# Sums and differences before the first stage, and the forward stage in bursts of 64x64 tiles

## The chip, the cores and the metric

The kernel runs on one core of a Trainium2 chip. The metric is the device time of one execution in microseconds (us), the median of several runs. Engines: TensorE (PE in the profile, its weight loads PEld), VectorE (DVE), ScalarE (ACT), GpSimd (POOL) and SyncE (SP); POOL and SP mostly issue DMA transfers here.

## The reference

Two parts follow one another. The first filters a sequence in the frequency domain, the second is a two-layer network with an exact GELU.

```python
X = np.fft.rfft(x, axis=1)                    # x: 8 batches, 3008 steps, 256 channels
Y = X * (filt_r + 1j * filt_i)[None]
y = np.fft.irfft(Y, n=3008, axis=1)
h = y.reshape(24064, 256) @ w_in              # 256 -> 2048
g = 0.5 * h * (1.0 + erf(h / sqrt(2)))
out = g @ w_out                               # 2048 -> 256
```

Inputs and output are fp32; the kernel works in bf16 and fp16 with fp32 sums in PSUM.

## The kernel before

**The transform.** 3008 = 47 x 64, so both transforms are done as small matrix products in two steps each. A step index is n = 64 n1 + 32 h + w. Per batch there are four stages on TensorE.

- s1 (lines 386 to 413): the sum over n1 (47 terms), one call for each quarter c of the 32 values of w. Its matmuls are 47 rows by 64 columns, so four of them, on two row halves and two column halves of the array, can stand side by side. Four PSUM banks are evicted into `a_sb`, which goes to DRAM (`R1`) and comes back in another order (r1).
- s2 (lines 421 to 431): the forward sum over the 64 values of (h, w), with the weights T2p. 24 matmuls of 128x128x256 per batch, two of them in each of 12 units p. VectorE multiplies each unit's PSUM bank by the filter F (line 430), real and imaginary part, and writes a tile `p12`.
- s3 (lines 434 to 458): the first inverse stage, 16 matmuls of 64x64x512 for each group u of four units, evicted to `v_sb` and turned through DRAM (`R2`, r2).
- s4 (lines 468 to 485): the last inverse stage; 16 calls per batch write the filtered sequence into a ring of two batches, `y_sb`.

Batch 0 goes another way, by transposes on chip (c1 to c4), in a start-up of about 39 us.

**The network.** 47 tiles of 512 tokens, each in 16 slots. In a slot, `mm1` (line 583) does two matmuls of 128x128x512 into a bank `ps_h` (three banks, which s1 and s3 also take one of), and ScalarE evicts it with GELU (line 595). `mm2_seven` does the second product of the tile before with seven instead of eight block products (Strassen's method): seven matmuls of 128x128x128 per slot into `ps_o` (two banks, line 665), 112 per tile in the order m = 0 to 6 of the block products, 16 each. VectorE prepares sums of quarters of g for it (`sums_1`, line 634, in slots 12, 13, 15 and 17; `sums_2`, line 640, in slots 16 and 18; `sums_3`, line 647, in slots 21 and 24, counted from the tile's own start) and combines the block products into the output (lines 680 to 694, after m = 0, 2, 4 and 6). A matmul of m = 2 needs sums_2: the 33rd matmul of a tile the first half, the 37th (slot 5) the second.

**Order.** The order is written out by hand: a table `at` puts each spectral call of batches 1 to 7 at a slot, and the loop at the end walks the slots and emits first the slot's table entries, then mm2, then mm1. Every engine executes in that order. For batches 3 to 6, with hi the first slot in which the batch is needed, s1 begins at hi - 94 and s2's units lie at about every third slot from hi - 70, with the three s3 bursts between them. Within one slot, entries stand in the order in which they were put: spectral calls of an earlier batch first, and the sums last.

**x.** One buffer holds x of a batch; GpSimd loads the next batch into it in eight transfers, each held back by a small copy (`gate`) that reads a product of s2.

Of the kernel before, what the change touches and what calls it, by code (L numbers as in the profile page):

```python
# [14 lines left out]
I32 = mybir.dt.int32  # L15
# [16 lines left out]
class _Mix:  # L32
    def __init__(self, ctx, tc, x, filt_r, filt_i, w_in, w_out, out):
# [12 lines left out]
        self.pp = pool("pp", 6)  # L46
# [11 lines left out]
        self.T2p = c.tile([128, K1, 2, 2, 2, 16], BF16, name="T2p")  # L58
# [20 lines left out]
    def load_x(self, b, lo=0, n=32, hs=(0, 1)):  # L79
        nc = self.nc  # L80
        if lo == 0 and 0 in hs:
            self.st[b, "x"] = self.px.tile([128 if b else 2 * NA, HB, 256], BF16, tag="x", name="x_sb")
        xt, o = self.st[b, "x"], 64 if b else NA
        xv = self.x[b].rearrange("(n1 h w) d -> h n1 w d", h=2, w=HB)
        for w in range(lo, lo + n, 8):
            for h in hs:
                nc.gpsimd.dma_start(out=xt[h * o:h * o + NA, w:w + 8, :], in_=xv[h][:, w:w + 8, :])  # L87

# [20 lines left out]
    def load_filters_again(self, eng, k0, k):  # L109

        for o in range(0, 128, 32):
            i = self.st["Fd"][o // 64, :, :, :, k0:k0 + k, :].rearrange("q i t k c -> (q i) t (k c)")
            eng.dma_start(out=self.F[o:o + 32, :, k0:k0 + k, :], in_=i)
# [11 lines left out]
    def load_next(self, b, p, c, h):  # L125

        if b > 0:
            self.gate(self.st[b, "p", p][0:1, 0, 0:1])
        self.load_x(b + 1, 8 * c, 8, (h,))
# [41 lines left out]
    def table_2_rows(self, g):  # L171


        v = self.nc.vector
        ts = v.tensor_scalar
        col = lambda name, dt=FP32: g.tile([128, 1], dt, name=name)
        ri_i, h_i, w_i = col("ri_i", I32), col("h_i", I32), col("w_i", I32)
        ts(out=h_i, in0=self.pi, scalar1=1, scalar2=1, op0=ALU.logical_shift_right, op1=ALU.bitwise_and)
        ts(out=w_i, in0=self.pi, scalar1=2, scalar2=None, op0=ALU.logical_shift_right)
        ts(out=ri_i, in0=self.pi, scalar1=1, scalar2=None, op0=ALU.bitwise_and)  # L180
        self.n2, self.ri = col("n2"), col("ri")
        v.scalar_tensor_tensor(out=self.n2, in0=h_i, scalar=float(HB), in1=w_i, op0=ALU.mult, op1=ALU.add)
        ts(out=self.n2, in0=self.n2, scalar1=1.0 / self.S, scalar2=None, op0=ALU.mult)
        ts(out=self.ri, in0=ri_i, scalar1=-0.25, scalar2=TURNS + 0.25, op0=ALU.mult, op1=ALU.add)
# [40 lines left out]
    def weights_4(self, g):  # L225

        ts = self.nc.gpsimd.tensor_scalar
        h, q, self.wt, self.wts = (g.tile([128, 1], FP32, name=n) for n in ("h48", "q48", "wt", "wts"))
        ts(out=h, in0=self.p, scalar1=48.0, scalar2=None, op0=ALU.is_ge)
        ts(out=q, in0=h, scalar1=-48.0, scalar2=-1.0, op0=ALU.mult, op1=ALU.add)  # L230
        self.nc.gpsimd.tensor_tensor(out=q, in0=self.p, in1=q, op=ALU.add)
        self.nc.gpsimd.tensor_tensor(out=q, in0=q, in1=q, op=ALU.mult)
        ts(out=q, in0=q, scalar1=1.0, scalar2=-1.0, op0=ALU.is_equal, op1=ALU.mult)
# [43 lines left out]
    def table_3_copy(self, q, turn):  # L277

        k = slice(8 * q, 8 * q + 8)
        if turn < 2:  # L280
            self._evac(self.T3[:, k], self.t3.rearrange("p (k w e) -> p k e w", k=8, e=4), "act")
        if turn:
            v = self.t3.rearrange("p (k w h r) -> p k h r w", k=8, h=2, r=2)
            for r in range(2):
                self._evac(self.T3i[:, k, r::2, :], v[:, :, :, 1 - r, :], "act", self.turn[r])

    def table_3_turn(self, q):

        k = slice(8 * q, 8 * q + 8)
        for r in range(2):  # L290
            self.nc.vector.tensor_scalar(out=self.T3i[:, k, r::2, :], in0=self.T3[:, k, 1 - r::2, :],
# [27 lines left out]
    def table_2_parities(self):  # L319
        t = self.T2.rearrange("p k r (s j e) -> p k r s j e", s=2, e=2)  # L320
        for par in range(2):
            for q in range(2):
                self.nc.gpsimd.tensor_copy(out=self.T2p[:, :, par, :, q, :], in_=t[:, :, :, q, :, par ^ q])

    def table_u_rows(self, g):
# [3 lines left out]
        v.tensor_copy(out=self.u0[:, 0], in_=self.T3[:, 0, 0:2, :])  # L329
        v.tensor_copy(out=self.u0[:, 1], in_=self.T3i[:, 0, 0:2, :])  # L330
# [14 lines left out]
    def table_4_rows(self, g):  # L345
# [5 lines left out]
        for x in range(2):  # L351
            for r in range(2):
                t = self.T1[0:NA, 24 * (x ^ r):24 * (x ^ r) + 24].rearrange("p (a k) -> p a k", k=2)
                v.tensor_copy(out=self.T1g[:, x, r], in_=t.unsqueeze(2).to_broadcast([NA, 12, 2, 2]))
        t = self.T2.rearrange("p (a k) r j -> p r a j k", k=2)[:, 0, :, 0:2, :]
        for r in range(2):
            v.tensor_copy(out=self.T2g[:, r], in_=t)

    def table_4_factors(self, g):
# [7 lines left out]
        self.fcs = t[:, 96:224].rearrange("p (w h r) -> p w h r", h=2, r=2)  # L367
# [16 lines left out]
    def s1(self, b, c):  # L384
# [4 lines left out]
        if b == 1 and c == 3:  # L389
            a = [self.pp.tile([128, 2, 512], BF16, tag="p12", name="p12") for i in range(2)]  # L390
        else:
            at = self.pa.tile([128, 4, 512], BF16, tag="a", name="a_sb")
            a = [at[:, 0:2], at[:, 2:4]]
        x = self.st[b, "x"]
        ps = [[self.bank("ps_s1", "h" if i == h == 0 else "f") for h in range(2)] for i in range(2)]
        for i in range(2):
            for r in range(2):
                for h in range(2):
                    w = 8 * c + 4 * r + 2 * i
                    nc.tensor.matmul(ps[i][h][64 * r:64 * r + 64, :], lhsT=self.T1s[64 * h:64 * h + NA],  # L400
                                     rhs=x[64 * h:64 * h + NA, w:w + 2, :], start=True, stop=True)
        for i in range(2):
            for h in range(2):
                self._evac(a[i][:, :, 256 * h:256 * h + 256], ps[i][h].rearrange("p (w c) -> p w c", w=2),
                           "act" if h and (b > 1 or i) else False)
        o = self.st[b, "R1"].rearrange("(w h) q c -> q w h c", h=2)
        for r in range(2):
            w, q = 8 * c + 4 * r, slice(64 * r, 64 * r + 48)
            if b == 1 and c == 3:
                for i in range(2):  # L410
                    nc.sync.dma_start(out=o[:, w + 2 * i:w + 2 * i + 2], in_=a[i][q].rearrange("q w (h c) -> q w h c", h=2))
            else:
                nc.sync.dma_start(out=o[:, w:w + 4], in_=at[q].rearrange("q w (h c) -> q w h c", h=2))
# [8 lines left out]
    def s2(self, b, p):  # L422
        nc = self.nc
        ps = self.bank("ps_s2")
        for i in range(2):
            k = 2 * p + i
            nc.tensor.matmul(ps[:, 256 * i:256 * i + 256], lhsT=self.T2p[:, k].rearrange("p a b c d -> p (a b c d)"),  # L427
                             rhs=self.st[b, "b", k // 6][:, k % 6, :], start=True, stop=True)
        w = self.st[b, "p", p] = self.pp.tile([128, 2, 512], BF16, tag="p12", name="p12")
        nc.vector.tensor_tensor(out=w, in0=ps.unsqueeze(1).to_broadcast([128, 2, 512]),  # L430
                                in1=self.F[:, :, 2 * p:2 * p + 2, :].rearrange("p t a b -> p t (a b)"), op=ALU.mult)
# [18 lines left out]
    def s3_out(self, b, u, i):  # L450
        ps = self.st[b, "ps3"][i]
        vt = self.pv.tile([128, 4, 256], BF16, tag="v", name="v_sb")
        for par in range(2):
            self._evac(vt[:, 2 * par:2 * par + 2, :].rearrange("p a b -> p (a b)"), ps[par],
                       "act" if par or b < 3 else False)
# [30 lines left out]
    def c1(self, grp, half, eng):  # L486

        if grp == 0 and half == 0:
            n = 4 * K1 * 2 * HB
            self.at = self.y0[:, 4608:4608 + n].rearrange("c (a k n h r) -> c a k n h r", a=2, k=K1, h=2, r=2)  # L490
        ps = self.bank("ps_c1", "n")
        x = self.st[0, "x"]
        for i in range(4):
            self.nc.tensor.matmul(ps[:, 96 * i:96 * i + 96], lhsT=x[:, 4 * grp + i, 128 * half:128 * half + 128],
                                  rhs=self.T1c, start=True, stop=True)
        self._evac(self.at[:, half].rearrange("c k n h r -> c k n (h r)")[:, :, 4 * grp:4 * grp + 4, :],
                   ps[:, 0:384].rearrange("c (i k e) -> c k i e", i=4, e=4), eng)

    def c1t(self, q, eng):
# [3 lines left out]
        for i in range(8):  # L503
            self.nc.tensor.transpose(ps[:, 128 * i:128 * i + 128],
                                     self.at[:, i % 2, 4 * q + i // 2].rearrange("c n h r -> c (n h r)"), self.eye)
# [4 lines left out]
    def c2(self, p):  # L510

        nc = self.nc
        w = self.st[0, "p", p] = self.pp.tile([128, 2, 512], BF16, tag="p12", name="p12")
# [220 lines left out]
def kernel(  # L734
# [20 lines left out]
    m.load_x(0, 0, 8)  # L755
    m.k48 = m.iota(g, "k48", [128, 2, K1], [[0, 2], [1, K1]])
    m.load_x(0, 8, 8, (0,))
# [5 lines left out]
    m.load_x(0, 8, 8, (1,))  # L763
    cols = m.cols = m.iota(g, "cols", [128, 128], [[1, 128]])
    m.load_x(0, 16, 16)
# [11 lines left out]
    t3 = m.pg.tile([128, 2, K1, 4, HB], BF16, tag="g", name="T3")  # L777
# [10 lines left out]
    for u in range(16):  # L788
        m.c1(u // 2, u % 2, False if u in (1, 3, 5, 7, 8, 10, 12, 14) else act)
        if u == 3:  # L790
# [4 lines left out]
            nc.vector.tensor_copy(out=m.T1q, in_=m.T1.rearrange("p (h r k) -> p k h r", h=2, r=2))  # L795
# [47 lines left out]
    m.load_x(1)  # L843
# [23 lines left out]
    for b in range(1, B):  # L867
        hi = first(b)
        if b == 1:
            s1, n1, r1, s2, n2, group = 0, 3, 12, 28, 3, 14  # L870
        elif b == 2:
            s1, n1, r1, s2, n2, group = hi - 87, 3.7, hi - 73, hi - 64, 3.4, 14
        else:
            s1, n1, r1, s2, n2, group = hi - 94, 3.7, hi - 80, hi - 70, 3.4, 14
        unit = lambda p: s2 + group * (p // 4) + int(n2 * (p % 4))
        busy.update(range(s1 - 1, s1 + int(3 * n1) + 2))
        for c in range(4):
            put(s1 + int(c * n1), m.s1, b, c)
            put(r1 if c < 3 else unit(3) + 1, m.r1, b, c)
        for p in range(12):  # L880
            put(unit(p), m.s2, b, p)
            busy.add(unit(p))
            if p % 4 == 3:
                put(unit(p) + 3, m.s3, b, p // 4)
                put(unit(p) + 4, m.s3_out, b, p // 4, 1)
                busy.update(range(unit(p) + 2, unit(p) + 6))
        after[b] = unit(11) + 7
        crowd.update(range(s2, after[b]))
        if b + 1 < B:
            for i in range(8):  # L890
                put(unit(i + 2), m.load_next, b, i + 2, i // 2, i % 2)

    for b in range(1, B):
# [8 lines left out]
        for u in range(7, -1, -1):  # L902
            due = (b * S + GRP * u) // TCH * 16
            end = min(end, due - 2 + 6 * (u == 0 and b == 1))
            for half in (1, 0):
                while end in busy:
                    end -= 1
                assert end > after[b] + 8
                put(end, m.s4, b, u, half, act if half or end in crowd or b == 1 and u == 0 else False)
                busy.add(end)  # L910
                end -= 2
            if u % 2 == 0:
                put(after[b] if u == 0 else end - 8, m.r2, b, u // 2)
# [65 lines left out]
```

## Time and profile before

| | |
|---|---|
| time, median of 3 runs | 745.92 us (745.81 to 746.71) |
| span of the profiled run | 745.3 us |
| PE busy | 728.5 us (98%) |
| DVE busy | 573.2 us (77%) |
| ACT busy | 557.5 us (75%) |
| POOL busy | 227.7 us (31%) |
| chain that ended last, share of PE | 91% |

Busy time is the union of an engine's instructions over the span. Rows of a group read: line, engine, operation, output and inputs, shape, count, then busy time, mean length of one in ns, and the engine's idle time before them with what ended it. TensorE's matmuls are pipelined: a matmul of 512 columns is recorded with 379 ns, but the next one starts 216 ns later. So the starts, not the lengths, tell what a matmul costs. The same holds, less strongly, for VectorE and ScalarE. A few per cent of the matmul records are missing.

### The profile page before, as it was taken

What the parts mean: (1) busy time and instruction counts of PE and PEld (TensorE: products, weight loads), DVE (VectorE), ACT (ScalarE), POOL (GpSimd) and SP (SyncE); (2) the same over time, 40 slices, a digit from 0 to 9 for tenths busy, and PEclk for the clock granted to TensorE, in tenths of its full rate; (3) what the DMA queues carried; (4) which work ended last, traced back from release to release, by engine and by line L of the source; (5) the groups of instructions that cost most, each with busy time, mean ns of one, the idle gap of its engine ahead of it and who ended that gap; (6) DMA issues with size and microseconds to landing.
All of it is one profiled execution on the core that took longest, in us unless ns stands there. A gap on an engine that the chain in (4) does not pass through costs nothing.

```text
span 745.3 us, 20244 instructions
## 1 busy us (share of the span) xinstructions
PE 728.5 (98%) x8287; PEld 518.7 (70%) x8420; DVE 573.2 (77%) x1028; ACT 557.5 (75%) x1000; POOL 227.7 (31%) x424
## 2 busy tenths in 40 slices
PE   7999999999999999999999999999999999999998
PEld 4856675766777776677777777677677766777776
DVE  7876877778678886789767996779957798676566
ACT  6996777777787777777777777877778777777773
POOL 7993216232312322133311342114311221112121
PEclk9999999999999999999999999999999999999999
DMA  8999743665266742657426654257533533401011
GB/s 140 218 234 244 141 97 102 190 113 132 68 162 154 141 98 72 171 143 133 122 64 172 135 112 123 71 157 145 125 100 94 145 111 92 117 29 58 30 58 58
DMA packets 76664, 90.74 MB, mean 122 GB/s; under 512 B 9755, under 2 KB 57883, under 8 KB 76315
## 3 DMA queue, kind: packets, MB, share of 16 engines
q1 hardware_dynamic: 58714, 49.63, 26.2%
q0 software_dynamic: 17440, 39.62, 24.2%
q8 instruction: 66, 1.08, 0.6%
q14 instruction: 28, 0.22, 0.1%
q10 hardware_dynamic: 416, 0.20, 0.1%
HBM read 57.15 MB, written 48.23 MB: 141 GB/s over the span
## 4 chain that ended last, share of the span: by engine, by line
PE 91%; DVE 2%; issue 2%; ACT 2%; DMA 2%; POOL 1%; DVEq 0%; POOLq 0%
PE ps_h L592 39%; PE ps_o L665 39%; PE ps_s L473 3%; PE ps_s L427 3%; PE ps_s L444 3%; PE ps_s L400 2%; ACT g_sb L595 1%; DMA x_sb<-in_x_dram 1%; PE ps_o L606 1%; DMA F<-in_filt_i_dram 1%; DVE p L521 1%; PE ps_c3t L554 1%; PE ps_c L539 0%; POOL x_sb L87 0%; DVE g_sb L640 0%
## 5 line engine op out<-in xcount | busy, mean ns | idle before, releaser
L595 ACT ACTIVATE g_sb<-ps_h 128x512 f16<-128x512 f32 x752 | 446.3, 600 | 166.8 <-PE ps_h L592 147.1
L592 PE MATMUL ps_h<-y_sb,w_in_sb 128*128 128x512 bf16 (+3 forms) x1471 | 417.5, 365 | 1.0
L665 PEld LDWEIGHTS <-g_sb 128*128 128x128 f16 x2944 | 194.8, 98 | 77.6 <-issue 12.8
L712 POOL DMA_DIRECT2D out_dram<-ost x221 | 125.0, 572 | 400.4 <-DVE ost L694 380.5
L665 PEld LDWEIGHTS <-s_sb 128*128 128x128 f16 x2208 | 148.7, 98 | 51.2 <-issue 5.8
L592 PEld LDWEIGHTS <-w_in_sb 128*128 128x128 bf16 x1600 | 125.0, 98 | 8.3 <-issue 1.7
L665 PE MATMUL ps_o<-w_sums,g_sb 128*128 128x128 f16 x1472 | 127.6, 219 | 2.0 <-DVE g_sb L640 0.9
L665 PE MATMUL ps_o<-w_sums,s_sb 128*128 128x128 f16 x1472 | 125.9, 219 | 0.9
L430 DVE TENSOR_TENSOR p<-ps_s,F 128x1024 bf16<-128x1024 f32 x84 | 102.4, 1220 | 26.8 <-PE ps_s L427 26.5
L634 DVE TENSOR_TENSOR s_sb<-g_sb 128x1024 f16<-128x1024 f16 x184 | 120.5, 683 | 1.0 <-ACT g_sb L595 1.0
L665 PE MATMUL ps_o<-w_out_sb,g_sb 128*128 128x128 f16 x1472 | 118.7, 219 | 0.9
L665 PE MATMUL ps_o<-w_out_sb,s_sb 128*128 128x128 f16 x736 | 63.8, 219 | 0.6
L640 DVE TENSOR_TENSOR g_sb<-s_sb,g_sb 128x1024 f16<-128x1024 f16 x92 | 63.1, 686 | 1.1
L647 DVE TENSOR_TENSOR s_sb<-g_sb 128x1024 f16<-128x1024 f16 x92 | 63.1, 686 | 0.0
L687 DVE TENSOR_TENSOR t_sb<-t_sb,ps_o 128x256 f32<-128x256 f32 x46 | 19.2, 418 | 46.5 <-PE ps_o L665 46.5
L473 PEld LDWEIGHTS <-d_sb 96*128 96x128 bf16 x448 | 31.9, 98 | 25.7
L306 DVE CAST a_sb<-ps_s 128x512 bf16<-128x512 f32 x57 | 36.6, 686 | 15.0 <-PE ps_s L400 14.9
L123 POOL COPY gate<-p 1x1 bf16<-1x1 bf16 x48 | 17.4, 363 | 96.8 <-DVE p L430 96.8
L682 DVE TENSOR_TENSOR ost<-t_sb,ps_o 128x256 f32<-128x256 f32 x46 | 19.2, 418 | 35.2 <-PE ps_o L665 35.0
L304 ACT ACTIVATE y_sb<-ps_s 128x376 bf16<-128x376 f32 x79 | 37.8, 479 | 2.6 <-PE ps_s L473 2.6
L473 PE MATMUL ps_s<-T4a,d_sb 96*128 96x94 bf16 x448 | 38.1, 206 | 1.1
L694 DVE TENSOR_TENSOR ost<-t_sb,ps_o 128x256 f32<-128x256 f32 x90 | 33.7, 415 | 6.6 <-PE ps_o L665 6.2
(149 smaller groups left out, 529.7 us busy)
## 6 DMA issues: line engine op xcount, KB each, us to landing
out_dram<-ost POOLq DMA_DIRECT2D x123, 128.0 KB, 2.2
x_sb<-in_x_dram POOLq DMA_DIRECT2D x64, 188.0 KB, 4.1
b_sb<-R SPq DMA_DIRECT2D x28, 384.0 KB, 4.1
R<-v_sb SPq DMA_DIRECT2D x84, 128.0 KB, 2.4
d_sb<-R SPq DMA_DIRECT2D x56, 192.0 KB, 4.5
R<-a_sb SPq DMA_DIRECT2D x54, 192.0 KB, 3.1
F<-Fd SPq DMA_DIRECT2D x4, 512.0 KB
Fd<-F SPq DMA_DIRECT2D x8, 192.0 KB, 7.2
```

The costliest lines, as they stand in the source:

```text
L304: self.nc.scalar.activation(out=out, in_=in_, func=AF.Copy, scale=1.0 if scale is None else scale)
L306: self.nc.vector.tensor_copy(out=out, in_=in_)
L430: nc.vector.tensor_tensor(out=w, in0=ps.unsqueeze(1).to_broadcast([128, 2, 512]), in1=self.F[:, :, 2 * p:2 * p + 2, :].rearrange("p t a b ...
L473: nc.tensor.matmul(ps[:, 94 * i:94 * i + 94], lhsT=d[:, (grp % 2) * 4 + i, 128 * half:128 * half + 128], rhs=self.T4a[:, 4 * grp + i], sta ...
L592: nc.tensor.matmul(ps[:, o:o + n], lhsT=w[:, dc], rhs=self.ring[:, dc, off:off + n], start=(dc == 0), stop=(dc == 1))
L595: nc.scalar.activation(out=self.st["g", t][:, jc, :], in_=ps, func=AF.Gelu)
L634: self.nc.vector.tensor_tensor(out=self.st["s", t][:, i:i + 2], in0=a, in1=b, op=ALU.subtract)
L640: self.nc.vector.tensor_tensor(out=a21[:, k], in0=self.st["s", t][:, k, 0], in1=a22[:, k], op=ALU.add)
L647: self.nc.vector.tensor_tensor(out=self.st["s4", t][:, k], in0=a12[:, k], in1=s2[:, k], op=ALU.subtract)
L665: nc.tensor.matmul(ps[:, (m + 1) % 2, sub, :], lhsT=a[:, i, 128 * sub:128 * sub + 128], rhs=b[:, i], start=i == 0, stop=i == 7)
L694: v(out=c(h, 1 - h), in0=tt, in1=p, op=ALU.add)
L712: eng.dma_start(out=out, in_=tile_[lo - r0:lo - r0 + n])
```

## The change

A real input lets the transform's even and odd outputs be taken from sums and differences of x(n) and x(n + 1504). x(n + 1504) is the value 23.5 rows of 64 on, so it lies in the other half h, 23 or 24 rows off.

- x is loaded in pairs: for each of the two halves v of w, the partner of each row lies in the same partition, one half of the buffer further on (`load_x_pairs`). From batch 2 on that is 24 transfers per batch in place of 8.
- `fold`: VectorE makes sum and difference, two operations of 111x1024 per quarter c, in place in the x buffer. s1 then takes the sums on one column half of the array and the differences on the other; its matmuls keep their shape and number.
- s2: each output is a sum over 64 rows of the sums or of the differences alone, so a 128x128 matmul becomes two of 64x64. 48 matmuls of 64x64x256 per batch, 16 of them in one burst for each u, into four banks; four products follow (`s2_out`), two slots apart. The inner count of columns per product stays.
- s1 evicts two of its four banks on ScalarE also for batch 1 (before: one), s3 all four on ScalarE (before, from batch 3 on: two on VectorE).
- The slots of s1, s2, s3, r2 and s4 move; tables for the start are laid out in another order; the filter copy for the second half of the partitions swaps neighbouring k.

```diff
-        self.pp = pool("pp", 6)
+        self.pp = pool("pp", 3)
...
+    def fold(self, b, c):
+        x, tt = self.st["x1"], self.nc.vector.tensor_tensor
+        k, n = slice(4 * c, 4 * c + 4), 64 + NA
+        s = self.st[b, "s", c] = x[:, 0, 4 * c - 4:4 * c] if c else self.xs
+        tt(out=s[0:n], in0=x[0:n, 0, k], in1=x[0:n, 1, k], op=ALU.add)
+        tt(out=x[0:n, 1, k], in0=x[0:n, 0, k], in1=x[0:n, 1, k], op=ALU.subtract)
...
-                           "act" if h and (b > 1 or i) else False)
+                self._evac(at[:, w:w + 2, :].rearrange("p w c -> p (w c)"), ps[i][v], "act" if v else False)
...
-    def s2(self, b, p):
-        ps = self.bank("ps_s2")
-        for i in range(2):
-            k = 2 * p + i
-            nc.tensor.matmul(ps[:, 256 * i:256 * i + 256], lhsT=self.T2p[:, k].rearrange("p a b c d -> p (a b c d)"),
-                             rhs=self.st[b, "b", k // 6][:, k % 6, :], start=True, stop=True)
+    def s2(self, b, u):
+        self.st[b, "ps2"] = ps = [[self.bank("ps_s2", "h" if i == d == 0 else "f") for d in range(2)] for i in range(2)]
+        for i in range(2):
+            for j in range(2):
+                for odd in range(2):
+                    for d in range(2):
+                        k, r = 8 * u + 4 * i + 2 * j + odd, slice(64 * d, 64 * d + 64)
+                        o = 64 * (odd ^ d)
+                        nc.tensor.matmul(ps[i][d][o:o + 64, 256 * j:256 * j + 256],
+                                         lhsT=self.T2p[r, k].rearrange("p a b c -> p (a b c)"),
+                                         rhs=self.st[b, "b", k // 6][r, k % 6, :], start=True, stop=True)
...
-                       "act" if par or b < 3 else False)
+                       "act")
...
-        if b == 1:
-            s1, n1, r1, s2, n2, group = 0, 3, 12, 28, 3, 14
-        elif b == 2:
-            s1, n1, r1, s2, n2, group = hi - 87, 3.7, hi - 73, hi - 64, 3.4, 14
-        else:
-            s1, n1, r1, s2, n2, group = hi - 94, 3.7, hi - 80, hi - 70, 3.4, 14
+        e = 4 * (b == B - 1)
+        s1, n1, r1 = (1, 4, 16) if b == 1 else (hi - 87, 3.7, hi - 73) if b == 2 else (hi - 94 - e, 3.7, hi - 80 - e)
+        s2 = (32, 46, 58) if b == 1 else (hi - 64 - 2 * e, hi - 48 - 3 * e, hi - 32 - 3 * e)
...
+            put(slot - 1 if b == 1 else s1 - 28 + 6 * c, m.fold, b, c)
+            put(slot, m.s1, b, c)
...
+        for u in range(3):
+            put(s2[u], m.s2, b, u)
+            for i in range(4):
+                put(s2[u] + 2 * i, m.s2_out, b, u, i // 2, i % 2)
+            put(s2[u] + 10, m.s3, b, u)
+            put(s2[u] + 11, m.s3_out, b, u, 1)
```

## The prediction

> **What bounds the kernel now.** I read the busy shares first.
>
> ```profile
> PE 728.5 (98%) x8287; PEld 518.7 (70%) x8420; DVE 573.2 (77%) x1028; ACT 557.5 (75%) x1000; POOL 227.7 (31%) x424
> ```
>
> TensorE (PE) is busy 98%, and the chain of waits gives it 91% of the span. A share alone could hide stalls, so next I asked what TensorE itself waited for: its largest wait inside the slot loop is this one.
>
> ```profile
> PE ps_o L665 <- DVE g_sb L640: 0.9, 2, 0.5
> ```
>
> 0.9 us in all. So in the slot loop the time is the sum of TensorE's instructions: every microsecond taken off TensorE is won, and every new stall is lost in full. The groups by shape give the three forward and inverse stages.
>
> ```profile
> L427 PE MATMUL ps_s<-b_sb,T2p 128*128 128x256 bf16 x168 | 32.1, 273 | 1.1
> L444 PE MATMUL ps_s<-p,U 64*64 64x512 bf16 x336 | 22.2, 382 | 0.6
> L400 PE MATMUL ps_s<-x_sb,T1s 47*64 47x512 bf16 x224 | 17.8, 388 | 0.3
> ```
>
> The means overlap, so the cost must be read as the distance of starts, in TensorE's timeline (start, length, ...):
>
> ```profile
> 262.92 0.59 PE L592 MATMUL ps_h<-y_sb,w_in_sb 128*128 128x512 bf16 x2
> 263.35 0.38 PE L427 MATMUL ps_s<-b_sb,T2p 128*128 128x256 bf16 x2
> 263.57 0.55 PE L665 MATMUL ps_o<-w_out_sb,g_sb 128*128 128x128 f16 x7
> 263.96 0.59 PE L592 MATMUL ps_h<-y_sb,w_in_sb 128*128 128x512 bf16 x2
> ...
> 265.61 0.59 PE L592 MATMUL ps_h<-y_sb,w_in_sb 128*128 128x512 bf16 x2
> 266.13 1.06 PE L444 MATMUL ps_s<-p,U 64*64 64x512 bf16 x16
> 267.12 0.56 PE L665 MATMUL ps_o<-w_out_sb,g_sb 128*128 128x128 f16 x7
> ```
>
> A plain slot is 0.39 (seven of mm2) + 0.43 (two of mm1) = 0.82 us. One s2 unit costs 263.57 - 263.35 = 0.22, so 0.11 per 256 columns and 0.216 per 512. An s3 burst: two mm1 end their stream at 265.61 + 0.43 = 266.04, the burst starts at 266.13, and the next 128-row work at 267.12. That is 1.08 us for 16 matmuls; four groups of four at 0.216 make 0.86, so entering and leaving the 64x64 shape costs 0.22.
>
> Last, the one tile that TensorE doesn't set, tile 0 (first row of busy times by stretch):
>
> ```profile
> 39.40:49.80 10.40, 10.26 (x67) 4.08 (x69) 9.40 (x15) 10.26 (x25) 10.04 (x17) 1.00 1.15 239
> ```
>
> ScalarE (the ACT column, 25 instructions) is busy 10.26 of 10.40 us. TensorE looks as busy only because its records overlap: 16 slots of mm1 and four s1 bursts need 16 x 0.43 + 4 x 0.65 = 9.5.
>
> **What the Trainium skill says.** "TensorEngine Tiling (Array Packing)", Key Properties: independent tiles work in parallel, and changing the tiling mode drains TensorE. The trace agrees: four 64x64 matmuls take the time of one, and a burst pays 0.22. "ScalarE: Activation LUTs", What ACT_TABLE_LOAD costs: back-to-back activations overlap by about 93 ns. Here it is more: in tile 0 eight GELUs take 4.23 us, so 0.48 to 0.5 each against 600 ns of the record. "VectorE: DVE Perf Modes", What auto-detection actually checks: two-source operations on 16-bit tensors with unit step reach two results per cycle. L634 does (683 ns for 1024), L430 with its fp32 PSUM source takes 1220; so a fold is priced like L634.
>
> **The change, part by part.**
>
> *s2 on TensorE.* Removed: 84 units x 0.218 = 18.3 us. Added: 21 bursts (7 batches x 3) of 16 matmuls of 64x64x256. No row shows this shape. Lower bound: four groups at 0.109 plus the 0.22 of an s3 burst, 0.655. Upper bound: weight loads for the next group don't fit under 256 columns and a group takes 0.216 as with 512: 1.08. I take the lower, because in s3 four loads (106 ns each) start together and the mm2 stream keeps 56 ns per matmul under loads of 98 ns. 21 x 0.655 = 13.8. Net **-4.5 us** (upper bound: +4.4).
>
> *Folds.* Two VectorE additions per quarter batch, 56 in all; by L634 0.60 start to start plus about 0.1 each for reading behind one another (L687 to L688 are 0.44 apart where independent ones of that size are 0.33), so 1.4 us a pair. Most stand in tiles without s2, beside TensorE's stream: nothing. Evictions of s3 move from VectorE to ScalarE (30 x 0.60 less on VectorE), where a burst of four finds a slack of 0.82 - 0.48 per slot and three PSUM banks: nothing.
>
> *Tile 0.* s1 of batch 1 evicted one of four banks per quarter on ScalarE, now two: 4 x 0.48 = 1.9 us on the engine that sets this tile. And s1 at slot 1 waits for the first fold, which waits on VectorE for the last c4 eviction (ends 39.8): the sum is there at 40.5, the difference at 41.2, evictions begin at 41.6, and ScalarE, done with GELU 0 at 40.5, idles 1.1. TensorE enters tile 1 up to three GELUs ahead, which gives back some 0.6. **+2.4** (bounds 1.6 and 3.2). If the six loads of the first half land later than 39.8 it is more; four of the old ones, equal in bytes, were issued from 30.6 and took 6.3 in the median.
>
> *VectorE's queue at a tile's start.* This is where I expect the new waits. The old trace has one such stall, on VectorE and on TensorE:
>
> ```profile
> 173.32 0.74 DVE L694 TENSOR_TENSOR ost<-t_sb,ps_o 128x256 f32<-128x256 f32 x2
> 173.99 0.68 DVE L640 TENSOR_TENSOR g_sb<-s_sb,g_sb 128x1024 f16<-128x1024 f16 x1
> 174.59 0.68 DVE L634 TENSOR_TENSOR s_sb<-g_sb 128x1024 f16<-128x1024 f16 x1
> 175.19 1.22 DVE L430 TENSOR_TENSOR p<-ps_s,F 128x1024 bf16<-128x1024 f32 x1
> 176.32 0.68 DVE L640 TENSOR_TENSOR g_sb<-s_sb,g_sb 128x1024 f16<-128x1024 f16 x1
> ```
>
> ```profile
> 176.49 0.22 PE L665 MATMUL ps_o<-w_sums,g_sb 128*128 128x128 f16 x1
> 177.06 0.51 PE L665 MATMUL ps_o<-w_sums,g_sb 128*128 128x128 f16 x6 [0.35 <-DVE g_sb L640]
> ```
>
> The 37th matmul of mm2 (slot 5) needs the second sums_2 (L640), and an s2 product of 1.135 (175.19 to 176.32) stands before it. I set up the same sum for each new burst, from the burst's first matmul. The first product starts at 0.45. In a usual batch (burst at slot 0): product 1.135, sums_2 0.60, sums_1 0.60, product 1.135, sums_2 0.68, so done at 4.6; TensorE asks at 0.56 + 5 x 0.82 + 0.06 = 4.7. It just fits; 15 bursts at 0 to 0.1, **+0.5**.
> Batch 1, second burst (slot 46, two before the tile): a product, sums_1, two combinations of 0.33, product, sums_2, sums_1, product, sums_2: done at 7.0, asked at 6.4: **+0.7**.
> Batch 1, third burst (slot 58) with the fold of batch 2 at slot 61: up to the two combinations after slot 15 there are three combinations (ready 1.8, 1.1), product, sums_1, fold 1.4, sums_1, product, sums_1, two combinations: 9.0. The bank they free is wanted in slot 18, at 0.56 + 8 x 0.82 + 0.11 = 7.25: **+1.8**; the s3 burst in slot 20 then hides the rest.
> Batch 6, third burst (slot 528): the fold of batch 7 at slot 530 stands ahead of the second sums_2: 4.6 + 1.4 = 6.0 against 4.7: **+1.3**.
> The stall shown above goes: **-0.5**.
>
> *DMA and POOL.* Twice the R1 stores at half the size, three times the x loads; 100 more issues at 0.53 us on a POOL that is busy 31%. Folds come 13 or more slots (11 us) after their loads, which landed in 4.1: nothing. Filter copies and table changes lie beside tiles 0 and 1: nothing.
>
> **Sum:** -4.5 + 2.4 + 0.5 + 0.7 + 1.8 + 1.3 - 0.5 = +1.7, so 745.9 + 1.7 = **747.6 us**.
>
> **Rivals.**
> 1. *Clear gain, 743.0.* The burst saves 4.5, of tile 0 only the four evictions stay (1.9), and VectorE finds gaps: 745.9 - 4.5 + 1.9 - 0.3. For it: VectorE's total rises little. Against: its queue is in order, and the stall shown follows my sum to 0.1 us.
> 2. *A draw, 745.5.* Half of the stalls (4.3 without the one that goes) come: 747.6 - 2.1. For it: each stall rests on an order of ten operations and shifts once TensorE is late.
> 3. *Weight loads set the s2 group.* +4.4 instead of -4.5: 747.6 + 8.9 = 756.5. Against: 106 ns of load against 109 of stream, and loads that start together.
>
> **Chances.** Forecast 0.45, rival 1 0.20, rival 2 0.30, rival 3 0.05. The range takes rival 1's end and the upper bounds of tile 0 and of the stalls, 743 to 752. Faster by over 0.2% (under 744.4): 0.20; within: 0.30; slower: 0.50.
>
> **What would show it.** s2 bursts 0.65 us apart from what follows them; GELU 15 of tile 0 two to three us later; TensorE waiting on VectorE for g_sb and for a freed ps_o bank, near slots 51, 66 and 533, some 4 us in all, against 0.9. It would be wrong if a group took over 0.15 us, if the first half of x(1) landed after 41, or if ScalarE fell behind after s3.

## The result, and the profile after

The changed kernel takes **751.02 us** (median of 4 runs, 750.57 to 751.36), the kernel before 745.88 beside it: a ratio of 1.0066, with a 95% interval of 1.0049 to 1.0083. It is slower by 5.1 us, where 1.7 was forecast. The time lies in the range (743 to 752), on the forecast side, but near its upper end, and 3.4 us of it are to be explained.

The busy shares of the changed kernel, first part of its page:

```profile
PE 724.9 (97%) x8450; PEld 507.4 (68%) x8588; DVE 581.7 (78%) x1034; ACT 574.7 (77%) x1050; POOL 287.6 (38%) x540
```

TensorE's busy time fell and the span rose: what was saved on TensorE came back as idle time of TensorE. VectorE and ScalarE gained 9 and 17 us of work, and neither is full. Who TensorE waits for is told by its waits (waited for: us in total, times, longest; the rows left out are waits of the start-up, of up to 1.4, and one of 0.6 for a GELU in tile 0):

```profile
PE ps_o L707 <- DVE g_sb L682: 2.2, 3, 1.2
PE ps_o L707 <- DVE ost L736: 1.9, 2, 1.7
...
PE ps_s L428 <- DVE xs L106: 0.9, 1, 0.9
...
PE ps_s L457 <- ACT v_sb L329: 0.4, 2, 0.2
PE ps_s L457 <- DMA b_sb<-R: 0.4, 1, 0.4
```

Before, the first row (L665, L640 there) was 0.9, in two waits, and the others were not in the list. L682 is `sums_2`, L736 the last combination of a tile, which frees a `ps_o` bank, L106 the sum that `fold` makes, L329 an eviction on ScalarE, L428 s1 and L457 the s2 burst.

**The burst itself** is as forecast. TensorE's timeline around one (start, length):

```profile
266.23 0.59 PE L634 MATMUL ps_h<-y_sb,w_in_sb 128*128 128x512 bf16 x2
266.76 0.63 PE L457 MATMUL ps_s<-b_sb,T2p 64*64 64x256 bf16 x16
267.32 0.56 PE L707 MATMUL ps_o<-w_out_sb,g_sb 128*128 128x128 f16 x7
```

Two mm1 end their stream at 266.23 + 0.43 = 266.66, and mm2 goes on at 267.32: 0.66 for a burst, against 0.655.

**Where the time goes, tile by tile.** I compared the start of each tile's first mm2 in both traces, counted from the last c4 matmul, because the profiled run of before came out of the start-up 1.26 us later than that of after. This is scatter as far as the traces show: that last c4 matmul starts at 39.22 before and at 38.40 in experiment 6, which has the same start-up, and at 37.7 to 38.7 in the traces with the change. After minus before, us:

| start of mm2 in tile | difference | what came in since the row above |
|---|---|---|
| 1 | +3.0 | tile 0 |
| 4 | +3.9 | the bursts of batch 1, with a stall of 0.68 and a bank wait |
| 6 | +6.0 | the stall at 99 (1.83), and 0.3 at the start of tile 5 |
| 10 | +5.6 | batch 2, with a wait for `b_sb` in one burst |
| 16 | +5.0 | batch 3 |
| 22 | +4.4 | batch 4 |
| 28 | +3.85 | batch 5 |
| 33 | +3.25 | two bursts of batch 6 |
| 34 | +4.6 | third burst of batch 6, stall at 541 |
| 47 | +4.7 | batch 7, with a bank wait |
| end of the trace | +5.0 | the last output transfer, issued 0.3 later |

So in the quiet batches 3 to 5 each three bursts win 0.6 us, and what is lost lies in tile 0 and in single waits in batches 1, 2, 6 and 7. Not every wait in the list is new. At the start of tile 5 the changed kernel waits 0.54 for `sums_2` (at 116.93), and the kernel before has the same wait:

```profile
112.36 0.51 PE L665 MATMUL ps_o<-w_sums,g_sb 128*128 128x128 f16 x6 [0.54 <-DVE g_sb L640]
```

It is 3.1 us into that tile there and 3.5 after the change, and it cancels in the table.

### The profile page after: what moved, and what is told of

It reads as the page before. It is cut to its first block, busy times and chain, and to the rows that moved or that the text cites. A ratio compares the mean times of both kernels' runs of the same rounds, so it can differ in the third digit from the quotient of the medians.

```text
span 749.0 us, 20863 instructions
## 1 busy us (share of the span) xinstructions
PE 724.9 (97%) x8450; PEld 507.4 (68%) x8588; DVE 581.7 (78%) x1034; ACT 574.7 (77%) x1050; POOL 287.6 (38%) x540
## 4 chain that ended last, share of the span: by engine, by line
PE 84%; ACT 5%; DVE 3%; DMA 3%; issue 2%; POOL 1%; DVEq 0%; SPq 0%; POOLq 0%
PE ps_o L707 36%; PE ps_h L634 36%; PE ps_s L483 3%; ACT g_sb L637 3%; PE ps_s L512 3%; PE ps_s L428 2%; DMA x_sb<-in_x_dram 2%; PE ps_s L457 1%; ACT v_sb L329 1%; PE ps_o L648 1%; DVE s_sb L676 1%; DMA F<-in_filt_i_dram 1%; ACT y_sb L329 1%; DMA b_sb<-R 1%; PE ps_c L581 0%
## 5 line engine op out<-in xcount | busy, mean ns | idle before, releaser
L98 POOL DMA_DIRECT2D x_sb<-in_x_dram x156 | 79.0, 513 | 0.7 <-PE ps_c3t L596 0.4
L682 DVE TENSOR_TENSOR g_sb<-s_sb,g_sb 128x1024 f16<-128x1024 f16 x92 | 65.1, 708 | 0.7
L329 ACT ACTIVATE y_sb<-ps_s 128x376 bf16<-128x376 f32 x95 | 47.3, 497 | 5.1 <-PE ps_s L512 5.1
L736 DVE TENSOR_TENSOR ost<-t_sb,ps_o 128x256 f32<-128x256 f32 x90 | 33.8, 417 | 21.9 <-PE ps_o L707 21.9
L331 DVE CAST a_sb<-ps_s 128x512 bf16<-128x512 f32 x54 | 34.8, 686 | 16.3 <-PE ps_s L428 16.0
L329 ACT ACTIVATE v_sb<-ps_s 128x512 bf16<-128x512 f32 x84 | 45.5, 597 | 0.2
```

Of the source, the lines that this page charges most:

```text
L98: self.nc.gpsimd.dma_start(out=xt[64 * v + to:64 * v + to + m, h, 4 * c:4 * c + 4 * n, :], in_=xv[h][at:at + m, w:w + 4 * n, :])
L329: self.nc.scalar.activation(out=out, in_=in_, func=AF.Copy, scale=1.0 if scale is None else scale)
L331: self.nc.vector.tensor_copy(out=out, in_=in_)
L682: self.nc.vector.tensor_tensor(out=a21[:, k], in0=self.st["s", t][:, k, 0], in1=a22[:, k], op=ALU.add)
```

## The experiments

Each time is given as the difference from the kernel before measured beside it (745.9 to 746.4): the changed kernel is at +5.1. My theory: the burst wins its 4 us; they are lost in tile 0 and to VectorE's in-order queue, where folds and products stand ahead of what TensorE asks for. The rivals: the burst costs more than counted; the folds cost everywhere; the transfers do it.

**1. Bursts twice.** Is the group of four tiles as cheap as it looks?

```diff
-        for i in range(2):
+        for i in (0, 1, 0, 1):
             for j in range(2):
```

> Each s2 burst computes its four groups twice over (the same values again), 84 groups more without one more change of shape. Theory (a group of four 64x64 tiles at 256 columns costs 0.109, an entry and exit 0.22): 84 x 0.109 = 9.2 more and up to 2 for products that start 0.45 later: 760 to 762. Rival (weight loads set the group at 0.2 or more, so that the bursts save nothing on TensorE): 768 or more.

760.29 us, +14.0, so 8.8 over the changed kernel (ratio to before 1.0189, interval 1.0175 to 1.0203). TensorE's timeline of this run:

```profile
269.60 0.59 PE L634 MATMUL ps_h<-y_sb,w_in_sb 128*128 128x512 bf16 x2
270.12 1.07 PE L457 MATMUL ps_s<-b_sb,T2p 64*64 64x256 bf16 x32
271.12 0.34 PE L707 MATMUL ps_o<-w_out_sb,g_sb 128*128 128x128 f16 x3
```

270.12 to 271.12 is 1.00, for the single burst it was 267.32 - 266.76 = 0.56. Four more groups of four tiles cost 0.44, 0.11 each, the same as one matmul of 128x128x256 in the kernel before. The weight loads hide, and the rival with dear groups is out. This agrees with what the Trainium skill says of independent tiles in "TensorEngine Tiling (Array Packing)", Key Properties, with 0.11 us for four.

**2. Folds left out.** s1 reads the halves of x as loaded; sums and differences are not made.

```diff
-        s = self.st[b, "s", c] = x[:, 0, 4 * c - 4:4 * c] if c else self.xs
-        tt(out=s[0:n], ...)
-        tt(out=x[0:n, 1, k], ...)
+        s = self.st[b, "s", c] = x[:, 0, k]
```

> The sums and differences are left out: s1 reads the two halves of x as loaded, so the output is another; loads, bursts and all else stay. Theory (folds cost through VectorE's queue and through s1's wait in tile 0): 3.3 as in the run with folds moved, and about 1.2 in tile 0: 746.5. Rival A (the loss is ScalarE's in tile 0 and the burst's own): 750 or more. Rival B (each of the 56 additions costs, by contention or delay everywhere): 743 or less.

746.08 us, ratio 0.9999 (0.9991 to 1.0008): 5.4 less than the changed kernel. The table of tile starts says where: tile 0 stands at +1.15 in place of +3.0, the stalls at 99 and 541 are shorter by 1.34 and 1.33, and batches 3 to 5 win the same 0.6 each as with folds. So the 32 additions of batches 3 to 6, all in quiet slots, cost nothing (rival B is out), and the others cost some 5: 1.9 in tile 0, 1.34 and 1.33 at the two stalls, and 0.3 at the start of tile 5.

**3. Folds of batches 2 and 7 moved, first try.**

```diff
-            put(slot - 1 if b == 1 else s1 - 28 + 6 * c, m.fold, b, c)
+            put(slot - 1 if b == 1 else s1 - 28 + 6 * c + {2: 9, 7: 4}.get(b, 0), m.fold, b, c)
```

> The folds of batch 2 nine slots later (70 to 88) and those of batch 7 four later (534 to 552), where the other batches have theirs in the tile. Theory (folds ahead of sums and combinations in VectorE's queue make TensorE's stalls): the stall at 99.1 loses the fold's 1.4 of 1.8, the one at 541.2 goes (1.3), the ones at 114 to 117 lose 0.7: 3.3 in all, so 747.7. Rival (these stalls come from the burst's own products or its bank and only show at the fold): at most 0.5 less, 750.5 to 751.

752.53 us (750.47 to 753.08), ratio 1.0080 (1.0067 to 1.0092): +6.2, slower still, a miss. Both stalls aimed at shrank as said (99 to 0.49, 541 to nothing). But the fold of slot 82 fell into tile 5, where mm1 pauses and mm2 runs at twice its pace, and TensorE waited 2.39 where it had waited 0.54:

```profile
117.61 0.82 PE L707 MATMUL ps_o<-w_sums,g_sb 128*128 128x128 f16 x6 [2.39 <-DVE g_sb L682]
```

and this wait had a sequel, in the stretches of the same trace (stretch, length, busy us and instructions of PE, PEld, DVE, ACT, POOL, then the granted clock):

```profile
115.00:118.00 3.00, 0.61 (x8) 0.44 (x6) 2.51 (x4) 0.00 (x0) 2.98 (x4) 0.81 0.47 160
118.00:120.00 2.00, 2.00 (x23) 2.00 (x21) 0.55 (x2) 0.48 (x1) 1.92 (x3) 0.50 0.00 0
124.00:126.00 2.00, 2.00 (x18) 1.10 (x16) 1.97 (x5) 1.94 (x5) 0.00 (x0) 1.00 0.00 0
```

After the wait, which ended at 117.61, TensorE ran at half its clock for about 6 us. The one of the five runs whose mean clock was 1.000 took 750.47, the four at 0.995 to 0.998 took 751.88 to 753.08.

**4. Folds moved, second try:** outside the start of tile 5.

```diff
+            put(slot - 1 if b == 1 else (68, 71, 74, 90)[c] if b == 2 else s1 - 28 + 6 * c + 4 * (b == 7), m.fold, b, c)
```

> The folds of batch 2 at slots 68, 71, 74 and 90, outside the dense start of tile 5 in which the run before had put one, those of batch 7 four slots later. Theory (folds ahead of sums and combinations in VectorE's queue): 1.3 less at 99, 1.3 less at 541, 0.7 less at 114 to 117, clock at 1.00: 747.7. Rival (VectorE is full there, so that a fold moved stalls TensorE elsewhere): 750 or more.

748.29 us, ratio 1.0027 (1.0019 to 1.0035): 3.2 less than the changed kernel, close to the sum that was expected (3.3). The parts fit less well. The stalls at 99 and 541 gave 1.3 each (now 0.49 at 99.8, none at 541), but the start of tile 5 only 0.3 of its 0.7: 0.39 + 0.70 are left at 115. Both are there without folds too (experiment 2), and the 0.70 is the old wait of the kernel before (recorded with 0.54), which no fold causes. The cause of the 0.39 I did not find.

**5. Tile 0: evictions back to VectorE.**

```diff
-                self._evac(at[...], ps[i][v], "act" if v else False)
+                self._evac(at[...], ps[i][v], "act" if v and (b > 1 or i) else False)
```

> In batch 1 one of four s1 banks is evicted on ScalarE again, as before the change, instead of two. Theory (tile 0 is set by ScalarE, four evictions of 0.48 too many): 1.9 less in tile 0, some of it given back by VectorE being later for the next fold: 749.1 to 749.7. Rival (s1 waits for the fold, and the evictions lie in the idle time this leaves on ScalarE): no change, 750.8 to 751.2.

752.70 us, ratio 1.0087 (1.0073 to 1.0101): +6.4, so 1.2 more, the opposite of what the theory said, and no rival said it either. Tile 0 stands at +4.5 in place of +3.0. VectorE is the later of the two engines here: the next fold stands behind three evictions (1.89 us) in its queue, and s1 waits for that fold.

```profile
43.41 0.40 PE L428 MATMUL ps_s<-x_sb,T1s 47*64 47x512 bf16 x2 [0.50 <-DVE x_sb L106]
```

The step "ScalarE sets tile 0, so four evictions off it are won" is wrong once the folds are there.

**6. Tile 0: the evictions alone,** in the kernel before.

```diff
-                           "act" if h and (b > 1 or i) else False)
+                           "act" if h else False)
```

> The kernel before with one edit: s1 of batch 1 evicts two of its four banks on ScalarE, as after the change. Theory (four evictions of 0.48 more on ScalarE, part of it given back when TensorE enters tile 1 ahead): 1.1 to 1.9 more than before. Rival (VectorE was the later of the two with three banks, so that sharing them evenly helps): 0 to 0.5 less than before.

747.72 us, ratio 1.0017 (1.0011 to 1.0024): +1.3, and from tile 0 on every tile starts 1.52 later in its trace, with no other change. So the extra evictions cost 1.3 to 1.5 without folds.

**7. Tile 0: folds ahead.**

```diff
+            put((0, 0, 4, 8)[c] if b == 1 else s1 - 28 + 6 * c, m.fold, b, c)
...
-        s1, n1, r1 = (1, 4, 16) if b == 1 else ...
+        s1, n1, r1 = (3, 3.7, 16) if b == 1 else ...
```

> In tile 0 the folds go to slots 0, 0, 4 and 8 and the four s1 of batch 1 to slots 3, 6, 10 and 14, so that each sum and difference is there before its s1; the evictions stay. Theory (s1's wait for the fold is 1.9 of tile 0's 3.0, as the run without folds has it): 1.5 to 1.9 less, 749.1 to 749.5. Rival (the wait only covers evictions that ScalarE must do anyway): 750.6 or more.

750.17 us, ratio 1.0050 (1.0036 to 1.0065): +3.8, so 1.4 won, just under the 1.5 to 1.9. In the trace tile 0 goes from +3.0 to +1.9, so 1.1 is won there, and 0.6 of it is lost again at the burst of slot 112, which waits longer for `b_sb`. s1 no longer waits for sums, but for 0.29 at the first difference; what is left is the evictions of experiment 6 and some.

**8. All moves together:** experiments 4 and 7, and the bursts

```diff
-        s2 = (32, 46, 58) if b == 1 else (hi - 64 - 2 * e, ...)
+        s2 = (32, 48, 60) if b == 1 else (hi - 64 + 2 * (b == 2) - 2 * e, ...)
```

> Folds placed, folds with a lead in tile 0, and bursts moved: the second and third of batch 1 to slots 48 and 60, the first of batch 2 to slot 114. Theory (the losses are separate waits and add up): 3.3 + 1.7 + 0.7 at slot 51 + 0.6 for the b_sb that lands late: 744.7, under the kernel before. Rival (with one wait gone VectorE's queue makes the next): 747 or more.

745.96 us, ratio 0.9997 (0.9989 to 1.0005): a draw with before, 5.6 less than the changed kernel, of 6.3 expected. The waits add up very nearly as separate ones. The stall at slot 51 and the wait for `b_sb` are gone; a stall of 0.80 at 99.9 is left.

**9. Bursts away from s3.** The bursts of slots 60 and 596 begin two slots after an s3 burst; they go one and two slots later (the last line leaves what follows the third burst at its slots).

```diff
-        s2 = (32, 48, 60) if b == 1 else (..., hi - 48 - 3 * e, ...)
+        s2 = (32, 48, 61) if b == 1 else (..., hi - 48 - 3 * e + e // 2, ...)
-        after[b] = s2[2] + 15
+        after[b] = s2[2] + 15 - (b == 1)
```

> As the run with all moves (s1 in tile 0), and the bursts of slots 60 and 596 moved to 61 and 598. Theory (the ninth matmul waits for a bank that ScalarE still empties of s3): 0.27 less twice and 0.2 at 99.9: 745.3 at a before of 746.3, under it. Rival (the wait moves on into VectorE's queue): 745.9 or more.

**744.45 us**, ratio 0.9972 (0.9963 to 0.9981): 1.9 less than the kernel before and 7.0 less than the changed one. Both waits inside the bursts are gone, and the stall at 100 is 0.64. The trace ends 0.8 earlier than that of experiment 8, counted from the last c4 matmul, as the theory's 0.7 has it; the profiled run is the slowest of its ten (745.11), with a wait of 1.0 for GpSimd in tile 0 that is 0.2 in experiment 8. Its busy shares and its largest wait for VectorE:

```profile
PE 722.2 (97%) x8448; PEld 506.7 (68%) x8588; DVE 580.6 (78%) x1035; ACT 574.5 (77%) x1049; POOL 288.9 (39%) x540
```

```profile
PE ps_o L707 <- DVE g_sb L682: 1.2, 3, 0.5
```

The work of every engine is that of the changed kernel to 0.5%; only its order differs, and the wait is down from 2.2, that for `ost` (1.9) gone.

**10 to 12. Two s1 of batch 1 into tile 1,** in three runs: on experiment 8 (first), with the spaced bursts of 9 (second), and with the filter loads of SyncE's queue at slot 21 in place of 17 (third). The load of `b_sb` moves from slot 16 to 20 in all three; the last two lines are of the third.

```diff
-        s1, n1, r1 = (1, 4, 16) if b == 1 else ...
+        s1, n1, r1 = (3, 5.4, 20) if b == 1 else ...
...
-            slot = s1 + int(c * n1)
+            slot = s1 + int(c * n1) if b > 1 else (3, 9, 16, 19)[c]
...
-    put(17, m.load_filters_again, nc.sync, 8, 16)
+    put(21, m.load_filters_again, nc.sync, 8, 16)
```

> The run with all moves, and besides the four s1 of batch 1 at slots 3, 9, 16 and 19 (two of them in tile 1), the folds at 0, 0, 6 and 12, the load of b_sb at 20. Theory (ScalarE sets tile 0, TensorE tile 1): four evictions of 0.48 leave tile 0, two s1 of 0.65 come to tile 1: 0.6 less than that run, 745.4. Rival (tile 0 is set by the order in TensorE's queue, which three GELUs of lead hide): no less, 745.9 or more.

> As the run with s1 in tile 1, and the two bursts that come two slots after an s3 burst (slots 60 and 596) one and two slots later. Theory (their ninth matmul waits for a PSUM bank that ScalarE is still emptying of s3): 0.27 less twice, 744.9. Rival (one slot more makes VectorE's products late for tile 4 or 38): 745.4 or more.

> As the run with spaced bursts, but the filter loads of SyncE's queue at slot 21, behind the loads of b_sb at 20, instead of 17, where they went ahead of the R1 stores and held the first s2 burst back by 9.5. Theory (that transfer was all that was wrong; ScalarE sets tile 0 and TensorE tile 1): 0.6 for the two s1 that leave tile 0 and 0.7 for the bursts less than the run with all moves: 744.7 at a before of 746.3. Rival (s1 in tile 1 costs what tile 0 gains, or b_sb is late still): 745.5 or more.

757.62 (ratio 1.0155, 1.0140 to 1.0170), 755.70 (1.0130, 1.0113 to 1.0146) and 745.04 us (0.9985, 0.9976 to 0.9994). The first two missed for a reason I had not thought of, a transfer. From the waits of the first of them:

```profile
PE ps_s L457 <- DMA b_sb<-R: 10.2, 2, 9.4
```

The filter transfers of slot 17 now stood ahead of the last four R1 stores in SyncE's queue. It took 10 us to issue them, and the stores came after:

```profile
54.75 9.99 SPq L139 DMA_DIRECT2D F<-Fd  x8
65.58 2.28 SPq L437 DMA_DIRECT2D R<-p  x4
```

In experiment 8 these stores were issued from 51.05 on. The load of `b_sb` that waits for them, and that the first burst needs, was issued at 70.98 in place of 57.22. With the filters behind (third run) the wait is gone. What is then left of the idea is nothing: tile 0 drops from +1.9 to +1.3, and tile 1 takes 0.9 more where before it took 0.2. So s1 costs TensorE in tile 1 what ScalarE saves in tile 0, as the rival had it. (The second run did cure both waits inside bursts, as in 9.)

## Why the prediction was right, and where it was short

**The sum.** Term by term, forecast and measured (from tile starts and stalls in the traces of both kernels):

| term | forecast | measured |
|---|---|---|
| s2 in bursts, with the waits of the usual ones | -4.5 + 0.5 = -4.0 | 7 x -0.6 = -4.2 |
| tile 0 | +2.4 | +3.0 |
| second burst of batch 1 | +0.7 | +0.68 |
| third burst of batch 1 with a fold | +1.8 | +1.83 |
| fold of batch 7 | +1.3 | +1.33 |
| old stall gone | -0.5 | -0.51 |
| start of tile 5, 113.5 to 117 | 0 | +0.3 |
| first burst of batch 2 waiting for `b_sb` | 0 | +0.7 |
| two bursts after s3 waiting for banks | 0 | +1.4 |
| last output transfer issued later | 0 | +0.3 |
| sum | +1.7 | +4.8; 5.0 in the two traces |

The medians differ by 5.1. Of the 3.1 that the sum is off, 2.7 were forecast at nothing and 0.6 belong to tile 0, less 0.2 that the bursts won beyond the forecast. The last row of terms stands behind the last matmul: from the start of mm2 in tile 47 on, both traces have the same matmuls at the same distances, but the last transfer is issued 7.40 after it in place of 7.09. All traces with the change end 0.3 to 0.5 later so; why, no run shows.

That the time fell into the range is in part luck. Its upper end was taken from larger stalls and a dearer tile 0, and most of what came on top, 2.7 us, came from elsewhere.

**What held.** The three stalls came where they were put and at their size, to 0.03 us; together they are 3.84, the "some 4 us" of the forecast. The third burst of batch 1 on VectorE's timeline:

```profile
95.90 0.68 DVE L676 TENSOR_TENSOR s_sb<-g_sb 128x1024 f16<-128x1024 f16 x1
96.50 0.69 DVE L106 TENSOR_TENSOR xs<-x_sb 111x1024 bf16<-111x1024 bf16 x1
97.22 0.69 DVE L107 TENSOR_TENSOR x_sb<-x_sb 111x1024 bf16<-111x1024 bf16 x1
97.83 0.69 DVE L676 TENSOR_TENSOR s_sb<-g_sb 128x1024 f16<-128x1024 f16 x1
98.43 1.22 DVE L469 TENSOR_TENSOR p<-ps_s,F 128x1024 bf16<-128x1024 f32 x1
99.56 0.68 DVE L676 TENSOR_TENSOR s_sb<-g_sb 128x1024 f16<-128x1024 f16 x1
100.16 0.75 DVE L736 TENSOR_TENSOR ost<-t_sb,ps_o 128x256 f32<-128x256 f32 x2
```

and on TensorE's:

```profile
99.03 0.28 PE L707 MATMUL ps_o<-w_out_sb,g_sb 128*128 128x128 f16 x2
100.96 0.45 PE L707 MATMUL ps_o<-w_out_sb,g_sb 128*128 128x128 f16 x5 [1.66 <-DVE ost L736]
```

VectorE has no gap from 95.90 to 100.9. The two folds (96.50 and 97.22) take 97.83 - 96.50 = 1.33 of it, and the combinations that free the bank come last. Experiment 4 took the folds away from here and the stall lost 1.34. The same sum, made for the fold of batch 7, gave 1.3 and was right to 0.03:

```profile
541.25 0.22 PE L707 MATMUL ps_o<-w_sums,g_sb 128*128 128x128 f16 x1
542.63 0.51 PE L707 MATMUL ps_o<-w_sums,g_sb 128*128 128x128 f16 x6 [1.17 <-DVE g_sb L682]
```

**Tile 0: mechanism right, size short.** Forecast were 1.9 for evictions, 1.1 for the wait on the first fold, less 0.6 given back. Measured are 1.5 for the evictions net of what is given back (experiment 6), where the forecast has 1.3, and 1.5 to 1.9 for the folds (experiment 2, and the rest of the 3.0), where it has 1.1. The mis-sized term is the wait: I counted it for the first fold only. On ScalarE it shows as forecast there:

```profile
40.47 1.08 ACT L329 ACTIVATE a_sb<-ps_s 128x512 bf16<-128x512 f32 x2 [1.17 <-PE ps_s L428]
```

1.17 idle against 1.1. But the next folds stand on VectorE behind evictions of the s1 before, so s1 at slots 5, 9 and 13 is late as well: 0.2 to 0.3 each between its sums and its differences.

**The step that failed: "DMA and POOL ... nothing", and "three PSUM banks: nothing", which measured 0.7 and 1.4.** Each was argued from what an engine or queue has to spare in all, not from what the burst needs at its start. A unit of the old s2 needed one `b_sb` and one bank at a time. A burst needs two `b_sb` and four banks at once. At slot 112 both loads came late: the first matmul waited 0.11, the second `b_sb` landed at 146.3, and the last four matmuls started 0.59 late (recorded with 0.42). The load itself is no slower than before: 4.0 us from issue to landing, and 4.2 in the kernel before, where its units ask for it later. And a burst two slots after an s3 burst finds two of its banks, those of the ninth and the tenth matmul, still being emptied by ScalarE:

```profile
602.23 0.69 PE L457 MATMUL ps_s<-b_sb,T2p 64*64 64x256 bf16 x9
603.13 0.41 PE L457 MATMUL ps_s<-b_sb,T2p 64*64 64x256 bf16 x7 [0.22 <-ACT v_sb L329]
603.48 0.40 PE L707 MATMUL ps_o<-w_out_sb,g_sb 128*128 128x128 f16 x4
```

```profile
602.00 1.08 ACT L329 ACTIVATE v_sb<-ps_s 128x512 bf16<-128x512 f32 x2
```

The wait is recorded with 0.22, but the burst takes 603.48 - 602.23 = 1.25 in place of 0.56, so 0.7 is lost. Its first two groups are through 0.22 after its start. The ninth matmul starts only at 602.64, when the first of ScalarE's two evictions is done, and the tenth, with the six behind it, at 603.13, when the second is (602.00 + 1.08 = 603.08); the recorded wait counts only from the end of the ninth. It happens twice, at slots 58 and 596. That s3 now evicts on ScalarE alone is not the reason: in batch 1, at slot 58, it did so before the change too. "ScalarE fell behind after s3" stood in the prediction as a sign of being wrong, but no cost was put to it. Experiment 8 moved the first kind by two slots, experiment 9 the second by one and two, and all three waits went.

**A misreading.** The prediction says that the old trace has one stall of TensorE on VectorE; its list of waits shows two, and the one left out is the larger, the 0.54 at 112.36. It lies just behind the last fold of batch 2, and the expectations of experiments 3 and 4 then took part of it for the folds' ("0.7 less at 114 to 117").

**"It just fits" was kinder than forecast.** In usual batches I allowed 0 to 0.1 for each burst at slot 0; the table of tile starts shows -0.6 per batch, against 3 x 0.655 - 12 x 0.218 = -0.65, so nearly nothing was lost there.

**The rivals.** The clear gain would have needed VectorE to find gaps; it finds them only where folds stand away from tile ends (experiments 4 and 8). The draw supposed that a late TensorE halves the stalls; none was halved. Dear weight loads are out by experiment 1.

## What to carry to other kernels

Where TensorE is full and VectorE's queue runs in order, price an added operation by its place: count what stands in the queue between the data and the operation that TensorE asks for next, and compare with the slot in which it asks; the same addition cost 0 in one slot and 1.3 us in another. When small units are joined into a burst, ask what the burst needs all at once (operands landed, banks free), not what the unit needed. And when such a change comes out slower, look first for the slots: here seven microseconds lay in the order alone, and with folds, bursts and s1 put elsewhere the change is worth 1.9 us (744.45 against 746.32).

## What the runs showed of the hardware

In two of these runs a wait of TensorE cost more than its length. After the wait of 1.66 us at 100 of the changed kernel the granted clock stayed at 1.00; after that of 2.39 us in experiment 3 it was 0.50 for some 6 us, and after the 9.4 us of experiment 10 it was low as well (stretch, length, busy us of the engines, granted clock):

```profile
75.00:80.00 5.00, 4.17 (x34) 2.66 (x30) 4.24 (x6) 0.80 (x2) 0.00 (x0) 0.54 0.74 251
```

In experiment 3 the clock fell during the wait. A mean of 0.81 in the three microseconds from 115 makes 1.1 us at 0.50, so it fell near 116.9, by this estimate 1.7 us after the wait began (117.61 - 2.39 = 115.22).

The Trainium skill tells of such a gate in "TensorE: Matmul & The Clock Gate", What's actually happening: two states, half and full, and a window of about 3.4 us of activity that decides. The two states agree. That a wait of 2.39 us was enough, shorter than the window, that section does not lead one to expect; the short wait ahead of it (0.26 at 113.6) may have counted, which no run here tells apart.
